# Attention scores in three units a batch instead of four, q in two transfers instead of four, and a new order of the work

## The chip, the cores and the metric

The kernel runs on one core of a Trainium2 chip. The core has a matrix engine (TensorE, PE in the profile, with its weight loads as PEld), a vector engine (VectorE, DVE), a scalar engine (ScalarE, ACT) and a general engine (GpSimd, POOL); SyncE (SP) issues DMAs. Each engine works through its own list of instructions in order and waits for the others by semaphores. The results of PE land in PSUM, eight banks of 512 fp32 columns on 128 partitions. The metric is the device time of one execution in microseconds (us), as the median of several executions.

## What is computed

Two stages, for 8 batches of 576 positions. First an attention of 8 heads of 64, whose keys and values are averages over 8 neighbouring positions (so 72 of them). Then a layer of four causal attention experts of width 64 over the result, of which the best two count at each position:

```python
k_p = k.reshape(B, H, Sp, pool, D).mean(axis=3)        # pool = 8, Sp = 72
v_p = v.reshape(B, H, Sp, pool, D).mean(axis=3)
attn = softmax(scale * np.matmul(q, k_p.transpose(0, 1, 3, 2)))
x = np.matmul(attn, v_p)                               # heads side by side: (8, 576, 512)
logits = x @ w_gate                                    # top 2 of 4 experts, softmax over them
for e in range(E):
    q, k, v = x @ wq[e], x @ wk[e], x @ wv[e]
    a = softmax(np.where(causal, -1e9, scale * (q @ k.transpose(0, 2, 1))))
    out += weight_of_expert_e * (a @ v @ wo[e])
```

(Shortened; `softmax` and the last line stand for several lines of the reference.)

## The kernel before, in words

The whole program is a list of short tokens, `SEQ` (from line 550), written out by a planner and replayed at the end of the kernel. A token is a name, its arguments, the batch, for PE work the PSUM bank (`@4`), and flags: `d` puts a read of PSUM on DVE instead of ACT, `c` cuts a PE step into four strips of 32 columns. Each engine executes its own tokens in the order of the list, so the order in `SEQ` is the order on every engine.

**Loads.** `L_q`, `L_k`, `L_v` are DMAs that POOL issues (`load`, line 114) and that convert fp32 to bf16; three raw buffers a tensor (`NRAW`). k and v come in three parts a batch, q in four: part c holds heads c and c + 4 on partitions 32c to 32c + 31. `W0` to `W4` load the weights: wq, wk, wv, the gate, wo; `c0` to `c4` copy them into order.

**First attention.** `PK` pools k on PE, `kc` copies it, `KT` transposes it, `kt` copies that into `kpT`. `U` (`turn`, line 252) transposes one head half of q on DVE into `qT`; a head half i is the four heads 4i to 4i + 3, one in each 32 partitions. `E` (`Es`, line 258) makes the scores of one head half and one half z of the positions, four heads side by side in the rows of the array and in four neighbouring banks, 288 columns each. `e` (`es`, line 268) reads the four banks and writes the exponentials into `eta` on ACT. `D` sums `eta` over the keys, `d` and `x` turn that into a reciprocal by a logarithm and an exponential on ACT. `PV`, `vc` pool v; `O` multiplies `eta` by it and `o` scales the result into `xT` on DVE. D0 and O0x take head half 0 of positions 0 to 511, D1 and O1x head half 1, D2 and O20 the last 64 positions of both.

**Experts.** `V` and `v` make the values and gate logits, `P` and `p` the queries and keys (q0, q1, k0, k1: of two experts each; t: the last 64 positions of all), `g` the gate, mostly on POOL. `S` makes expert scores, `s` their exponentials on ACT, `a` the causal mask on POOL. `B` multiplies by the values, `bz` (DVE), `bg` (POOL) and `b` (DVE) scale. `T` and `t` transpose, `Y` multiplies by wo, `y` copies into an output tile, which SP sends off (the very last tile also ACT, in two halves `ya`, `yb`).

`H` is a run of matmuls without use that keeps PE busy at the start (39 in all).

Of the kernel before, what the change touches and what calls it, by code (L numbers as in the profile page):

```python
# [20 lines left out]
def kernel(  # L21
# [12 lines left out]
    nc = tc.nc  # L34

    B, H, S, D = q.shape
# [17 lines left out]
    NRAW = 3  # L54
    KR = 96
    NRG = 4
    NTK = S // 32
    HALF = S // 2
# [12 lines left out]
    psum = psp.tile([128, 8, 512], FP32, name="psum")  # L71
# [4 lines left out]
    qraws = bufs(NRAW, [128, 2, NTK, D], BF16, "qraw")  # L76
# [3 lines left out]
    kpTs = bufs(2, [128, 2, 2, KR], BF16, "kpT")  # L80
# [33 lines left out]
    def load(b, nm, c):  # L114
        if nm == "q":
            dst = qraws[b % NRAW][32 * c : 32 * c + 32].rearrange("p e s d -> p e (s d)")
            src = q[b, c::NRG, :, :].rearrange("e (p s) d -> p e (s d)", s=NTK)
        else:
            raw, T = (kraws, k) if nm == "k" else (vraws, v)
            dst = raw[b % NRAW][:, c, :, :, :].rearrange("p h t d -> p h (t d)")  # L120
            src = T[b, :, 2 * KR * c : 2 * KR * (c + 1), :].rearrange("h (p t) d -> p h (t d)", t=2)
        nc.gpsimd.dma_start(out=dst, in_=src)  # L122
# [135 lines left out]
    def Es(b, bank, i, z):  # L258
        for u in range(2):
            for r in range(NRG):  # L260
                rows = slice(32 * r, 32 * r + 32)
                nc.tensor.matmul(  # L262
                    out=psum[0:KR, bank + r, 0 : HALF].rearrange("j (s x) -> j s x", s=NTK),
                    lhsT=kpTs[b % 2][rows, u, i, :], rhs=qTs[b % 2][rows, i, :, 16 * z : 16 * z + 16, u],
                    start=(u == 0), stop=(u == 1), tile_position=(32 * r, 0),
                )

    def es(b, bank, dve, i, z):
        nc.scalar.activation(  # L269
            out=etas[b % 2][:, NRG * i : NRG * i + NRG, HALF * z : HALF * z + HALF].rearrange(  # L270
                "j r (x s) -> j r x s", s=NTK),
            in_=psum[0:KR, bank : bank + NRG, 0 : HALF].rearrange("j r (s x) -> j r x s", s=NTK),
            func=EXP, scale=ATT_EXP_SCALE,
        )
# [260 lines left out]
    def z(b, c, queue):  # L535
# [15 lines left out]
        I:0 L_k1:0 L_k2:0 L_k0:0 J:0 K:0 H16:0@7 PK:0@2 kc:0 H4:0@7 KT:0@7 kt:0 L_q2:0 L_q3:0 L_q0:0  # L551
        L_q1:0 U0:0 H7:0@6 E00:0@4 L_q1:1 L_k2:1 L_k0:1 L_k1:1 L_q3:1 L_q0:1 e00:0 E01:0@0 U1:0
        E11:0@4 e01:0 D0:0@0 e11:0 d0:0 x0:0 PK:1@1 kc:1d L_q2:1 E10:0@4 H2:0@3 KT:1@2 e10:0 H4:0@3
        D1:0@4 kt:1 U1:1 E10:1@0 L_v2:0 d1:0 L_v1:0 H2:0@7 E11:1@4 e10:1 U0:1 E01:1@0 e11:1 e01:1
        D2:0@4 d2:0 L_v0:0 PV:0@5 W3:0 vc:0 D1:1@6 E00:1@0 x1:0 M:0 H1:0@7 O11:0@5 O01:0@4 o11:0
        d1:1 L_v0:1 e00:1 L_v1:1 O10:0@7 o10:0 O00:0@6 o00:0 L_v2:1 PV:1@5 vc:1 W0:0 D0:1@2 c0:0d
        H3:0@7 O20:1@5 W1:0 L_k1:2 W2:0 o01:0 x2:0 O11:1@6 d0:1 c1:0 c2:0d O00:1@3 O01:1@0 x0:1
        o00:1 D2:1@2 d2:1 O10:1@1 o01:1 x1:1 x2:1 L_k2:2 c3:0 P_q0:0@4c o20:1 p_q0:0 P_k0:0@2c
        O20:0@3 o20:0 p_k0:0 o10:1 P_q1:0@7c o11:1 L_k0:2 c4:0 L_q1:2 S00:0@2 P_t0:0@5c L_q0:2
        P_k1:0@4c L_q3:2 L_q2:2 p_t0:0d L_q1:3 V1:0@5c p_q1:0d PK:2@7 s00:0 p_k1:0 S12:0@3 S10:0@1  # L560
        kc:2d L_k1:3 V0:0@6 L_k0:3 v1:0d s12:0 v0:0d L_k2:3 KT:2@7 V2:0@0 kt:2d U0:2 L_q3:3 L_v1:2
        s10:0 L_q2:3 L_q0:3 S03:0@3 s03:0 L_k1:4 V3:0@5 v3:0 L_v0:2 S02:0@6 v2:0d L_v2:2 g0:0 g1:0
        E01:2@1 V0:1@5 P_k0:1@0 e01:2 E00:2@1 s02:0 v0:1d L_v1:3 p_k0:1d P_k1:1@5 U1:2 p_k1:1d e00:2
        S11:0@6 PK:3@0 L_v0:3 E10:2@1 s11:0 a00:0 kc:3d P_q1:1@5c L_v2:3 e10:2 D0:2@0 p_q1:1d KT:3@6
        E11:2@1 L_q1:4 a11:0 L_k2:4 P_t0:1@7 d0:2 L_k0:4 V4:1@0 V1:1@5 kt:3d L_q2:4 U0:3 p_t0:1d
        v1:1d e11:2 E00:3@1 x0:2 L_q3:4 v4:1 S01:0@6 V2:1@0 V3:1@5 U1:3 g2:0 v2:1d e00:3 E10:3@1
        s01:0 v3:1d L_q0:4 e10:3 L_q1:5 PV:2@0 D2:2@5 D1:2@6 d1:2 g1:1 d2:2 L_v0:4 P_q0:1@7c x1:2
        E01:3@1 e01:3 L_v1:4 vc:2d L_q0:5 O11:2@0 p_q0:1d o11:2 S12:1@5 L_k2:5 O00:2@7 O10:2@0
        L_k0:6 o00:2 D0:3@1 s12:1 o10:2 g3:0 O01:2@2 o01:2 g4:0 g5:0 g6:0 L_v2:4 d0:3 PV:3@3 E11:3@4
        x2:2 vc:3d L_v2:6 g7:0 S10:1@0 P_q1:2@2c p_q1:2d e11:3 L_k2:6 a01:0 a03:0 g8:0 s10:1 a10:0  # L570
        O20:2@3 S03:1@4 s03:1 D1:3@6 x0:3 o20:2 PK:4@7 kc:4d S01:1@0 s01:1 g2:1 g3:1 g4:1 a12:1
        S00:1@4 V2:2@3 v2:2d P_t0:2@2 V3:2@7 KT:4@3 s00:1 S11:1@0 p_t0:2d d1:3 L_q3:5 P_k0:2@2 s11:1
        U0:4 g0:1 kt:4d E00:4@3 a01:1 v3:2d e00:4 g5:1 g6:1 O01:3@7 D2:3@0 d2:3 P_k1:2@1c L_k0:5
        p_k0:2d x1:3 O00:3@2 g9:0 o01:3 O10:3@7 p_k1:2 g7:1 L_q1:6 E01:4@3 L_q0:6 U1:4 a12:0
        P_q0:2@0c g8:1 O11:3@1 a02:0 o10:3 e01:4 V1:2@7c o00:3 E11:4@3 V0:2@2c o11:3 V1:3@1c p_q0:2d
        L_q2:5 x2:3 L_k1:5 L_q3:7 e11:4 L_q3:6 a11:1 v0:2d v1:3d v1:2d V2:3@0c O20:3@2 g9:1 E10:4@3
        v2:3d e10:4 o20:3 B11:0@1 bz11:0 B01:0@7 bz01:0 bg01:0 B10:0@2 bg11:0 S02:1@3 S03:2@5 s03:2
        P_k0:3@0c s02:1 bz10:0 bg10:0 b10:0 D1:4@5 L_q2:7 V0:3@6c a00:1 L_k1:6 L_v2:5 PV:4@2 PK:5@3
        d1:4 L_v0:5 p_k0:3 v0:3 b11:0 U1:5 S12:2@4 s12:2 x1:4 b01:0 L_v1:5 vc:4d kc:5d S02:2@0
        S10:2@6 s10:2 a02:1 V3:3@2 V4:3@3 v4:3d B00:0@4 s02:2 bz00:0 bg00:0 v3:3d P_k1:3@5 T1:0@3  # L580
        D0:4@6 d0:4 a10:1 g0:3 PK:6@2 D2:4@7 L_v1:7 d2:4 b00:0 S01:2@0 s01:2 t1:0d S11:2@3 T0:0@6
        t0:0 a03:1 B11:1@7 kc:6d s11:2 p_k1:3d B01:1@2 x0:4 a02:2 x2:4 KT:5@5 g1:2 g2:2 P_q0:3@0
        bz11:1 bz01:1 P_t0:3@1 kt:5d E11:5@3 bg11:1 b11:1 p_t0:3 bg01:1 L_q2:6 B00:1@7 p_q0:3d b01:1
        L_v2:7 e11:5 S02:3@0 s02:3 g3:2 g1:3 g2:3 P_q1:3@2 bz00:1 bg00:1 U0:5 b00:1 a10:2 p_q1:3d
        g0:2 a01:2 E01:5@3 g4:2 L_q1:7 KT:6@7 kt:6d O00:4@0 o00:4 g3:3 g4:3 S01:3@1 O01:4@7 e01:5
        o01:4 L_k2:7 L_v0:6 L_k1:7 s01:3 E00:5@3 e00:5 O10:4@0 o10:4 S00:2@1 s00:2 O20:4@7 o20:4
# [110 lines left out]
```

## Time and profile before

| | us |
|---|---|
| median of 8 executions | 171.14 (170.43 to 172.31) |
| the profiled execution | 172.1 |
| its span on the core | 170.4 |
| first use of k on PE | 8.36 |
| first score on PE | 12.60 |
| first projection (`P_q0:0`) on PE | 29.57 |
| last matmul ends | 165.29 |
| ACT reads of scores (line 269) | 32, busy 35.8, mean 1132 ns |
| score matmuls (line 262) | 256, busy 15.4 |
| q issues on POOL | 32, busy 17.5, mean 550 ns |

The profile is of one execution. Its page gives busy times of each engine, a row of digits for each engine over 40 slices of the span (9 is 90% or more), the chain of work that ended last, and groups of instructions: line, engine, operation, tiles, count, then busy time and mean, then idle time before them and what ended it. The timeline lists instructions in order of time: start, duration, engine, line, and in square brackets the idle time before it and its cause. The table by stages gives the busy time of PE, PEld, DVE, ACT and POOL in a stretch (number of instructions in brackets), then the granted clock of PE, and DMA's share and rate.

The DMA queue of the loads moved 15.21 MB (counted as written). PE's idle time by stages: 6.7 us in the first 30 us, 5.0 between 30 and 100 us, none from 100 to 165 us.

### The profile page before, as it was taken

To read this page: it belongs to the slowest core of one execution; us is meant where nothing else is said; L and a number is where in the kernel's file an instruction comes from. 1 tells how busy PE (TensorE), PEld (TensorE's weight loads), DVE (VectorE), ACT (ScalarE), POOL (GpSimd) and SP (SyncE) were. 2 spreads that over 40 slices of the span, in tenths; PEclk is the share of its full clock that TensorE was granted. 3 is DMA by queue.
4 is the path that set the end of the run, shared out by engine and by line. 5 is a ranking of instruction groups with operands and counts; after the bars stand their busy time and mean duration, and the time that the engine had idled before them with its cause. 6 is when DMAs were issued, how large, how long until landed. Compare 5 with 4: busy or idle time off the path is not lost.

```text
span 170.4 us, 6329 instructions
## 1 busy us (share of the span) xinstructions
PE 153.6 (90%) x2625; PEld 84.0 (49%) x2625; DVE 110.7 (65%) x291; ACT 133.6 (78%) x226; POOL 108.6 (64%) x262
## 2 busy tenths in 40 slices
PE   7576979989999897979999899999999999999980
PEld 2232333444543544746546347645666675546740
DVE  1121706857778659668897587875995577868760
ACT  3029599959999994669999899889679859699880
POOL 7977873588957899988999316523405347456610
PEclk9996599999999999999999999999999999999997
DMA  2999999999999999999799901011530144377795
GB/s 23 167 177 195 177 181 180 202 185 191 182 189 195 181 128 117 148 151 149 86 100 150 162 6 67 4 62 65 206 112 0 65 123 153 105 263 290 230 339 177
DMA packets 49132, 25.05 MB, mean 147 GB/s; under 512 B 42192, under 2 KB 42448, under 8 KB 49104
## 3 DMA queue, kind: packets, MB, share of 16 engines
q0 software_dynamic: 43856, 15.21, 79.0%
q1 hardware_dynamic: 5168, 9.31, 15.4%
q8 instruction: 20, 0.33, 0.8%
q10 hardware_dynamic: 80, 0.13, 0.4%
q14 instruction: 8, 0.07, 0.1%
HBM read 30.42 MB, written 9.44 MB: 234 GB/s over the span
## 4 chain that ended last, share of the span: by engine, by line
PE 61%; POOL 12%; DMA 11%; ACT 8%; issue 3%; DVE 1%; POOLq 0%; DVEq 0%
PE psum L191 53%; DMA kraw<-in_k_dram 8%; ACT eta L269 6%; POOL kraw L122 4%; PE psum L262 4%; DMA qraw<-in_q_dram 3%; PE psum L200 3%; POOL qraw L122 2%; POOL etb L449 2%; PE psum L179 2%; ACT etb L432 2%; POOL vraw L122 1%; DVE qT L253 0%; ACT rza L295 0%; POOL Df L359 0%
## 5 line engine op out<-in xcount | busy, mean ns | idle before, releaser
L432 ACT ACTIVATE etb<-psum 128x1024 bf16<-128x1024 f32 x48 | 48.2, 1029 | 5.8 <-PE psum L191 5.0
L269 ACT ACTIVATE eta<-psum 96x1152 bf16<-96x1152 f32 x32 | 35.8, 1132 | 7.9 <-PE psum L262 7.6
L449 POOL TENSOR_SCALAR_AFFINE_SELECT etb<-etb 128x256 bf16<-128x256 bf16 x64 | 24.9, 406 | 8.0 <-ACT etb L432 7.5
L317 DVE TENSOR_TENSOR xT<-psum,rza 128x512 bf16<-128x512 f32 x32 | 20.6, 682 | 7.1 <-PE psum L191 5.2
L191 PE MATMUL psum<-wvg,xT 128*32 128x260 bf16 (+1 forms) x372 | 20.9, 275 | 1.9 <-DVE xT L317 1.2
L122 POOL DMA_DIRECT2D kraw<-in_k_dram x24 | 18.9, 792 | 4.4 <-PE psum L191 2.3
L182 DVE CAST qk<-psum 128x512 bf16<-128x512 f32 (+1 forms) x26 | 16.7, 647 | 6.8 <-PE psum L191 5.9
L191 PE MATMUL psum<-xT,wkp 128*32 128x512 bf16 (+3 forms) x308 | 20.4, 299 | 0.8 <-issue 0.8
L122 POOL DMA_DIRECT2D qraw<-in_q_dram x32 | 17.5, 550 | 5.1 <-DMA oT<-in_moe_wk_dram 1.0
L191 PE MATMUL psum<-xT,wqp 128*32 128x512 bf16 (+3 forms) x320 | 20.1, 301 | 0.6 <-issue 0.6
L122 POOL DMA_DIRECT2D vraw<-in_v_dram x24 | 18.6, 781 | 3.1 <-DMA qraw<-in_q_dram 1.3
L191 PE MATMUL psum<-wop,oT 128*128 128x512 bf16 (+2 forms) x98 | 20.1, 375 | 0.0
L191 PEld LDWEIGHTS <-etb 128*128 128x128 bf16 x480 | 17.3, 97 | 4.7 <-issue 2.0
L191 PE MATMUL psum<-vaug,etb 128*128 128x65 bf16 x480 | 19.0, 193 | 0.0
L262 PE MATMUL psum<-qT,kpT 32*96 32x288 bf16 x256 | 15.4, 317 | 2.5 <-ACT eta L269 1.4
L488 DVE TENSOR_TENSOR osc<-psum,gt 128x256 bf16<-128x256 f32 (+2 forms) x36 | 15.4, 440 | 3.1 <-POOL gt L483 3.1
L191 PE MATMUL psum<-qk 64*128 64x64 bf16 (+4 forms) x192 | 17.3, 278 | 0.1
L191 PEld LDWEIGHTS <-xT 128*32 128x32 bf16 (+1 forms) x372 | 13.9, 96 | 6.8 <-issue 4.2
L253 DVE STREAM_TRANSPOSE qT<-qraw 128x576 uint32<-128x576 uint32 x16 | 12.1, 765 | 8.0 <-DMA qraw<-in_q_dram 7.5
L483 POOL TENSOR_TENSOR gt<-rzb,G 128x4 f32<-128x4 f32 (+2 forms) x36 | 6.9, 201 | 15.1 <-DVE rzb L481 14.8
L182 DVE COPY ofin<-psum 128x512 f32<-128x512 f32 (+1 forms) x20 | 13.4, 674 | 3.4 <-PE psum L191 2.6
L191 PE MATMUL psum<-eta,vp 96*32 96x64 bf16 (+1 forms) x256 | 13.8, 288 | 0.4 <-DVE xT L317 0.3
(78 smaller groups left out, 234.4 us busy)
## 6 DMA issues: line engine op xcount, KB each, us to landing
out_dram<-ofin SPq DMA_DIRECT2D x32, 256.0 KB, 2.2
kraw<-in_k_dram POOLq DMA_DIRECT2D x24, 192.0 KB, 6.1
qraw<-in_q_dram POOLq DMA_DIRECT2D x32, 144.0 KB, 6.4
vraw<-in_v_dram POOLq DMA_DIRECT2D x24, 192.0 KB, 6.4
out_dram<-ofin SPq DMA_DIRECT2D x7, 128.0 KB, 2.3
oT<-in_moe_wq_dram POOLq DMA_DIRECT2D x1, 256.0 KB, 8.1
oT<-in_moe_wk_dram POOLq DMA_DIRECT2D x1, 256.0 KB, 8.7
oT<-in_moe_wv_dram POOLq DMA_DIRECT2D x1, 256.0 KB, 9.0
```

Of the source, the lines that this page charges most:

```text
L122: nc.gpsimd.dma_start(out=dst, in_=src)
L182: (nc.vector.tensor_copy if dve else nc.scalar.copy)(out=out, in_=in_)
L191: nc.tensor.matmul(out=out, lhsT=lhsT, rhs=rhs, start=start, stop=stop)
L200: nc.tensor.transpose(out=out[s], in_=in_[:, s], identity=ident[0:n, 0:n])
L253: nc.vector.transpose(out=qTs[b % 2][:, i].rearrange("p s x u -> p (s x u)").bitcast(U32), in_=qraws[b % NRAW][:, i].rearrange("p s d -> p ...
L262: nc.tensor.matmul(out=psum[0:KR, bank + r, 0 : HALF].rearrange("j (s x) -> j s x", s=NTK), lhsT=kpTs[b % 2][rows, u, i, :], rhs=qTs[b % 2 ...
L269: nc.scalar.activation(out=etas[b % 2][:, NRG * i : NRG * i + NRG, HALF * z : HALF * z + HALF].rearrange("j r (x s) -> j r x s", s=NTK), i ...
L317: nc.vector.tensor_tensor(out=xT[:, 2 * g + t, mcols(b)], in0=psum[:, bank, :], in1=rz[:, g, 0:MAIN], op=MULT)
L432: nc.scalar.activation(out=et[:, ep, :, eo : eo + n], in_=psum[:, bank : bank + 2, 0:n], func=EXP, scale=MOE_EXP_SCALE,)
L449: nc.gpsimd.affine_select(out=blk, in_=blk, pattern=[[0, 2], [1, 128]], compare_op=ISGE, fill=0.0, base=0, channel_multiplier=-1,)
L483: nc.gpsimd.tensor_mul(out=gt[:, :, :, 0], in0=rz[:, :, :, 0], in1=at[b // 2, "G"][:, p0:p1, 2 * ep : 2 * ep + 2].rearrange("p c e -> p e c"),
L488: nc.vector.tensor_tensor(out=oscs[ep][:, own, :].rearrange("p c (e d) -> p e c d", e=2), in0=o[:, :, :, 0:HD], in1=gt.to_broadcast([128, ...
```

## The change

Scores: the 2 x 576 columns of the two head halves are cut at columns 378 and, in the second half, 180. The first unit takes 378 columns of half 0, the second the other 198 of half 0 and 180 of half 1 side by side in the same four banks, the third the last 396 of half 1. ACT still reads four pieces a batch, of 4 x 378, 198, 180 and 396 columns; `e10` now reads what `E01` wrote. There is no `E10`.

Queries: a transfer c is head half c of all 128 partitions (288 KB as written, 144 KB before), two a batch, so that `U0` waits for one transfer and `U1` for the other.

```diff
     def load(b, nm, c):
         if nm == "q":
-            dst = qraws[b % NRAW][32 * c : 32 * c + 32].rearrange("p e s d -> p e (s d)")
-            src = q[b, c::NRG, :, :].rearrange("e (p s) d -> p e (s d)", s=NTK)
+            dst = qraws[b % NRAW][:, c].rearrange("p s d -> p (s d)")
+            src = q[b, NRG * c : NRG * c + NRG, :, :].rearrange("r (p s) d -> (r p) (s d)", s=NTK)
...
-    def Es(b, bank, i, z):
-        for u in range(2):
-            for r in range(NRG):
-                rows = slice(32 * r, 32 * r + 32)
-                nc.tensor.matmul(
-                    out=psum[0:KR, bank + r, 0 : HALF].rearrange("j (s x) -> j s x", s=NTK),
-                    lhsT=kpTs[b % 2][rows, u, i, :], rhs=qTs[b % 2][rows, i, :, 16 * z : 16 * z + 16, u],
-                    start=(u == 0), stop=(u == 1), tile_position=(32 * r, 0),
-                )
+    XCUT = {(0, 0): (0, 21), (0, 1): (21, 32), (1, 0): (0, 10), (1, 1): (10, 32)}
+    UNITS = {(0, 0): [(0, 0)], (0, 1): [(0, 1), (1, 0)], (1, 1): [(1, 1)]}
+
+    def xpart(i, z):
+        x0, x1 = XCUT[i, z]
+        off = NTK * (XCUT[0, 1][1] - XCUT[0, 1][0]) if (i, z) == (1, 0) else 0
+        return x0, x1, slice(off, off + NTK * (x1 - x0))
+
+    def Es(b, bank, *unit):
+        for i, z in UNITS[unit]:
+            x0, x1, cols = xpart(i, z)
+            for u in range(2):
+                for r in range(NRG):
+                    rows = slice(32 * r, 32 * r + 32)
+                    nc.tensor.matmul(
+                        out=psum[0:KR, bank + r, cols].rearrange("j (s x) -> j s x", s=NTK),
+                        lhsT=kpTs[b % 2][rows, u, i, :], rhs=qTs[b % 2][rows, i, :, x0:x1, u],
+                        start=(u == 0), stop=(u == 1), tile_position=(32 * r, 0),
+                    )
 
     def es(b, bank, dve, i, z):
+        x0, x1, cols = xpart(i, z)
         nc.scalar.activation(
-            out=etas[b % 2][:, NRG * i : NRG * i + NRG, HALF * z : HALF * z + HALF].rearrange(
+            out=etas[b % 2][:, NRG * i : NRG * i + NRG, NTK * x0 : NTK * x1].rearrange(
                 "j r (x s) -> j r x s", s=NTK),
-            in_=psum[0:KR, bank : bank + NRG, 0 : HALF].rearrange("j r (s x) -> j r x s", s=NTK),
+            in_=psum[0:KR, bank : bank + NRG, cols].rearrange("j r (s x) -> j r x s", s=NTK),
             func=EXP, scale=ATT_EXP_SCALE,
         )
```

The order: all of `SEQ` is planned anew. Its head and its end, old and new:

```diff
-        I:0 L_k1:0 L_k2:0 L_k0:0 J:0 K:0 H16:0@7 PK:0@2 kc:0 H4:0@7 KT:0@7 kt:0 L_q2:0 L_q3:0 L_q0:0
-        L_q1:0 U0:0 H7:0@6 E00:0@4 L_q1:1 L_k2:1 L_k0:1 L_k1:1 L_q3:1 L_q0:1 e00:0 E01:0@0 U1:0
-        E11:0@4 e01:0 D0:0@0 e11:0 d0:0 x0:0 PK:1@1 kc:1d L_q2:1 E10:0@4 H2:0@3 KT:1@2 e10:0 H4:0@3
-        D1:0@4 kt:1 U1:1 E10:1@0 L_v2:0 d1:0 L_v1:0 H2:0@7 E11:1@4 e10:1 U0:1 E01:1@0 e11:1 e01:1
-        D2:0@4 d2:0 L_v0:0 PV:0@5 W3:0 vc:0 D1:1@6 E00:1@0 x1:0 M:0 H1:0@7 O11:0@5 O01:0@4 o11:0
-        d1:1 L_v0:1 e00:1 L_v1:1 O10:0@7 o10:0 O00:0@6 o00:0 L_v2:1 PV:1@5 vc:1 W0:0 D0:1@2 c0:0d
...
-        Y3:6@6 b11:7 t02:6 bg01:7 B02:7@0 bz02:7 b01:7 Y1:7@3 y3:6 B12:7@2 t12:6 bz12:7 T11:7@1
-        bg02:7 y1:7 T01:7@4 t01:7 b02:7 Y0:7@5 y0:7 t11:7d bg12:7 b12:7 T02:7@0 t02:7d Y2:7@1 y2:7d
-        T12:7@6 t12:7 Y3:7@3 y3:7 Y4:7@4 ya4:7 yb4:7d
+        I:0 L_k1:0 L_k0:0 J:0 L_k2:0 K:0 H16:0@7 PK:0@6 kc:0 H4:0@7 KT:0@6 M:0 L_q0:0 U0:0 L_q1:0
+        kt:0d H3:0@7 E00:0@4 e00:0 U1:0 L_k1:1 L_k0:1 H1:0@3 E01:0@0 e01:0 E11:0@4 e10:0 e11:0
+        L_k2:1 PK:1@0 D0:0@3 H2:0@2 D1:0@7 kc:1d L_q1:1 d0:0 U1:1 KT:1@2 L_q0:1 L_v1:0 d1:0 kt:1d
+        D2:0@4 H2:0@6 E11:1@0 U0:1 d2:0 E00:1@4 e11:1 e00:1 L_v2:0 L_v0:0 E01:1@0 e01:1 PV:0@4 vc:0
+        H4:0@7 O11:0@7 L_k0:2 O10:0@5 O00:0@4 e10:1 D1:1@0 W3:0 x0:0 D0:1@2 o00:0 L_k1:2 L_k2:2
+        O01:0@1 o01:0 D2:1@3 W0:0 x1:0 H2:0@6 PK:2@6 o11:0 L_q1:2 kc:2 o10:0 x2:0 W2:0 c0:0 L_q0:2
+        c1:0d O20:0@4 o20:0 H4:0@1 KT:2@6 kt:2d H1:0@7 P_q1:0@7 d1:1 d2:1 W1:0 U1:2 L_v0:1 L_v2:1
+        x1:1 p_q1:0d H3:0@6 E11:2@3 d0:1 L_v1:1 e11:2 c4:0d x2:1 P_q0:0@0 p_q0:0 U0:2 V2:0@2 V0:0@7
+        v2:0 L_k2:3 V3:0@1 L_k1:3 E01:2@3 v0:0d c3:0d L_k0:3 V1:0@7 x0:1 e10:2 L_q1:3 v3:0d e01:2
+        P_k1:0@2 c2:0d L_v2:2 P_t0:0@1 L_q0:3 v1:0 p_t0:0 E00:2@3 P_k0:0@7c D1:2@1 p_k1:0d p_k0:0d
+        e00:2 d1:2 PV:1@2 D0:2@3 d0:2 L_v1:2 S01:0@6 vc:1d S11:0@0 L_v0:2 O00:1@4 o00:1 L_k2:4 s01:0
...
+        bg12:7 b12:7 a12:7 bg02:7 b02:7 bz01:7 B11:7@2 bg01:7 Y0:7@0 t02:6d bz11:7 bg11:7 b01:7
+        T12:7@3 T02:7@1 t02:7d y3:6 Y1:7@4 t12:7d y0:7 Y4:7@5 b11:7 T11:7@3 t11:7 y1:7d ya4:7 yb4:7d
+        T01:7@2 t01:7d Y3:7@2 y3:7 Y2:7@7 y2:7
```

In the new list, PE has the same steps but for the scores (24 instead of 32) and `H` (42 matmuls instead of 39). Between ACT and DVE reads have moved: `y` on ACT 22 instead of 16, `v` 12 (10), `p` 15 (14), `kc` 2 (1), `kt` 1 (2), `t` 8 (12), weight orders `c` 1 (3); DVE has the rest. POOL issues 64 loads instead of 80.

In the replay, `e10` looks up the bank of `E01`:

```diff
-                fn(b, at[b, src, a], bool(dve), *a, **({"later": True} if later else {}))
+                fn(b, at[b, src, (0, 1) if name == "e" and a == (1, 0) else a], bool(dve), *a, **({"later": True} if later else {}))
```

## The prediction

> **What bounds the kernel now.** I read the page first: engine shares, then the slices, then the chain that ended last.
>
> ```profile
> PE 153.6 (90%) x2625; PEld 84.0 (49%) x2625; DVE 110.7 (65%) x291; ACT 133.6 (78%) x226; POOL 108.6 (64%) x262
> ...
> PE   7576979989999897979999899999999999999980
> ...
> POOL 7977873588957899988999316523405347456610
> PEclk9996599999999999999999999999999999999997
> DMA  2999999999999999999799901011530144377795
> ...
> PE 61%; POOL 12%; DMA 11%; ACT 8%; issue 3%; DVE 1%; POOLq 0%; DVEq 0%
> ```
>
> Three stages show. From slice 2 to 19 (4 to 81 us) the DMA row stands at 9: the inputs arrive as fast as the queue lets them. POOL, which issues them, is fullest from 60 to 90 us. From slice 24 on PE is full to the end; the table by stages has PE busy 10.00 of 10 us in every stretch from 100 to 160. So the time is: how late PE gets going, plus its work, plus what it loses before 100 us, plus the tail. ACT is close behind (9.81 of 10 us busy in both 40:50 and 50:60).
>
> **1. The score units on PE.** Per batch there were four units of 8 matmuls with 288 columns; there will be three, of 8 x 378, 8 x 198 + 8 x 180, and 8 x 396. Matmuls (256) and columns stay; the starts and ends of units fall from 32 to 24. A unit's price stands in the timeline of PE:
>
> ```profile
> 40.31 0.59 PE L191 MATMUL psum<-xT,wkp 128*128 128x512 bf16 x2
> 40.84 0.47 PE L262 MATMUL psum<-qT,kpT 32*96 32x288 bf16 x8
> 41.24 1.04 PE L191 MATMUL psum<-xT,wkp 128*128 128x512 bf16 x4
> ```
>
> The four of the last line run 3 steps in 1.04 - 0.38 = 0.66 us (0.38 is one's own duration), so 512 columns stream in 0.22 us and 288 in 0.12. The first line's pair has streamed by 40.31 + 0.43 = 40.74; the unit starts at 40.84 and the next work at 41.24. Two passes of 0.12 leave 0.10 us ahead of the unit and 0.16 within and behind it; its start times show 0.04 of that between the passes. A boundary thus costs 0.22 us; one goes, and one gap between passes (0.04) comes. Saved: 0.18 us a batch, 1.4 in all. Only where PE sets the pace does this count; batches 0 to 2 are scored while DMA does. I take 5.5 batches, **-1.0 us** (bounds 0 and -1.4).
>
> On ACT the four reads a batch stay. From 128x512 in 607 ns and 96x1152 in 1132 the slope is 0.82 ns a column: 1512, 792, 720 and 1584 columns make 1.43 + 0.84 + 0.78 + 1.49 = 4.53 us, against 4 x 1.13 = 4.53. Nothing. The middle unit holds its four banks for 1.62 us instead of 1.13, but three holdings sum to the same 4.5: nothing, in the sum. The unit E01 now needs both halves of qT, a new wait; in batch 0, E11, PK:1 and D0 queue behind it on PE.
>
> **2. The start.** Now the first turn waits for all four q transfers:
>
> ```profile
> 11.77 1.44 DVE L253 STREAM_TRANSPOSE qT<-qraw 128x576 uint32<-128x576 uint32 x2 [6.71 <-DMA qraw<-in_q_dram]
> ...
> 12.60 0.74 PE L262 MATMUL psum<-qT,kpT 32*96 32x288 bf16 x16 [0.94 <-DVE qT L253]
> ...
> 13.12 1.13 ACT L269 ACTIVATE eta<-psum 96x1152 bf16<-96x1152 f32 x1 [2.46 <-PE psum L262]
> ```
>
> The landing marks of batch 0: third k at 8.32, the q parts at 9.24, 9.97, 10.69, 11.64, that is 0.83 us each. In the new form a transfer is one head half, twice the bytes: q0 lands at 8.32 + 1.65 = 10.0, q1 still at 11.6. Then U0 0.77, kt on DVE behind it 0.35, E00 0.5: first exponential at 11.7, 1.4 us earlier. U1 ends at 12.4, E01 at 13.0, before e00 ends at 13.2: the new wait costs nothing here, ACT covers it. M's memsets (1.3 us on DVE) now come ahead of U0, where DVE waits for q anyway. ACT then runs 4.5 us without a break, and the eta of batch 0 is whole at 16.3 against 18.6. The next gate is v of batch 0, landed at 21.1 in both orders (same bytes ahead of it); PV, vc, O and o follow at once, and the first projection starts at about 27.2 to 27.7, against 29.57.
>
> From there the bytes decide. The new order puts all of k for batch 2 and most of its q ahead of weight W1 and of v of batch 1. At the measured 0.18 MB/us W2 lands at 29.5 (30.35 before), W1 at 32.9 (27.8 before). So P_k1:0 waits until 33, and V and E01 of batch 2 fill in before it. Walking PE's order with its step times (P 0.87, V 0.45, D and O 0.22, PK 0.54), PV:1 is done at 36.5 with 15.9 us of work in old prices behind it; the old order had 14.4 at that time. Ahead by 1.5 us at most; ACT, at 9.81 of 10 from 40 us on, passes on only a part. I take **-0.8 us** (bounds 0 and -1.5).
>
> A **rule** stands against this part. The Trainium skill, "TensorE: Matmul & The Clock Gate", section on the HAM clock gate, says that the array's clock falls to half after an idle window of about 3.4 us and rises only after a busy one, the windows running freely. The trace agrees, in steps of 3.41 us:
>
> ```profile
> 7.57:10.98 3.41, 2.62 (x19) 1.18 (x19) 0.00 (x0) 1.06 (x2) 2.69 (x6) 1.00 1.09 182
> 10.98:14.39 3.41, 1.51 (x24) 0.85 (x25) 1.44 (x2) 1.27 (x2) 2.69 (x4) 1.00 1.67 175
> 14.39:17.80 3.41, 3.06 (x28) 0.93 (x28) 0.69 (x1) 3.32 (x5) 2.74 (x5) 0.50 1.38 197
> 17.80:21.22 3.42, 3.42 (x22) 1.24 (x20) 2.65 (x10) 1.48 (x3) 2.97 (x4) 0.50 1.89 177
> ```
>
> First number after the comma: PE busy; third from the end: granted clock. 1.51 us of work lost the full clock at 14.4; 3.06 did not bring it back, 3.42 did at 21.2, and the warm-up matmuls H2 and H4 were what filled that window. In the new order 17.8:21.2 holds D1, KT:1, D2, E11, E00, E01 and two warm-up matmuls, with waits for ACT between: my walk fills some 2.6 us. By the row's own clock my start stands; by the rule half clock lasts one window longer, to 24.6, and slows PV, H4 and O by some 0.5 us, which the wait for W1 then swallows. I take the walk, and keep the longer half clock as a rival.
>
> **3. Fewer transfers.** 32 q issues become 16.
>
> ```profile
> L122 POOL DMA_DIRECT2D kraw<-in_k_dram x24 | 18.9, 792 | 4.4 <-PE psum L191 2.3
> ...
> L122 POOL DMA_DIRECT2D qraw<-in_q_dram x32 | 17.5, 550 | 5.1 <-DMA oT<-in_moe_wk_dram 1.0
> ```
>
> The new transfer has 128 rows instead of 64: between 550 ns and the gate weights' 720 (256 rows); by rows, 610. 16 x 0.61 = 9.8, so POOL is relieved of 7.7 us. What does it carry to the end? Between 60 and 75 us the chain runs through POOL into a late k for batch 5:
>
> ```profile
> 73.82 0.63 PE L191 MATMUL psum<-kraw,poolk 96*32 96x512 bf16 x5 [0.97 <-DMA kraw<-in_k_dram]
> ```
>
> That 0.97 us is PE's only visible wait for a load there; q issues are 2% of the chain, 3.9 us, and 45% of that would go. So 0 to -1.8; **-0.9**, because next behind the load stand waits for xT (1.2 us) that the change does not touch. On the transfers themselves the skill ("DMA: Bandwidth & Descriptors", anatomy of one DMA on the SWDGE path) gives each about 2.0 us fixed: by it 16 fewer would free 32 us of queue. The landings say otherwise: 144 KB parts land 0.72 to 0.96 us apart, the fixed part hidden behind those in flight. I put nothing.
>
> **4. The tail.** Now the last reads are short and the PE never waits:
>
> ```profile
> 164.26 1.03 PE L191 MATMUL psum<-wop,oT 128*128 128x512 bf16 x6
> ...
> 165.38 0.42 DVE L182 COPY ofin<-psum 128x256 f32<-128x256 f32 x1 [0.29 <-PE psum L191]
> ```
>
> PE ends at 165.29, the last copy at 165.81. In the new order T01 follows Y4 and T11, and t01 stands on DVE behind y1 (0.69) and yb4 (0.42). From the start s of Y1: y1 until s+1.3, yb4 until 1.7, t01 until 2.0; PE is out of work from 1.2. Y3 runs at 2.05, Y2 at 2.5, and y3, y2 follow each other on ACT (0.59 each) until 3.8. Work ends 0.8 us later than with a full PE, and the last copy 0.3 us farther behind. **+1.1 us** (bounds 0.4 and 1.4).
>
> **5. Moves between ACT and DVE.** Six more y (0.585) go to ACT, +3.5; v +1.1, p +0.6, kc +0.6; away go t 2.4, weight orders 1.9, kt 0.5. ACT +1.0 us of 133.6, DVE -3.7 of 110.7. Priced at nothing while PE is fuller than ACT; where ACT is full it is the second rival below. Three more warm-up matmuls (42 for 39) lie in waits.
>
> **Sum.** -1.0 - 0.8 - 0.9 + 1.1 = -1.6 on a span of 170.4: 168.8. Outside the span lie 172.1 - 170.4 = 1.7, so 170.5 beside the profiled execution's 172.1; from the median of 171.14 it is **169.5**. All low bounds give -4.3, all high ones +1.4: 166.8 to 172.5.
>
> **The rivals.**
> - **Everything carries through** (0.22): start and units count in full, the POOL relief too, -1.5 - 1.4 - 1.8 + 1.1 = -3.6: 167.5. For it: PE is full from 100 us on, so what is won earlier stays. Against: ACT at 98% in the middle.
> - **ACT takes over** (0.17): between 40 and 100 us ACT runs without gaps, its list is 1.0 longer, so the -0.8 and the unit savings vanish there; -0.9 - 0.3 + 1.1, about 0: 171.0. It is also the case in which the units save nothing.
> - **Half clock lasts into the projections** (0.17), the slower case. It decides if the window 21.2:24.6 is not filled either. Then 24.6:31.4 runs at half rate; 7 us of windows do 3.5 us less, from which the -1.6 is already taken: 170.4 - 1.6 + 3.5 = 172.3 in the span, 173.0. For it: warm-ups come in pieces of 1 to 4 between waits. Against: from 21.1 v has landed and PE has O, D and PK in a row.
> - Forecast: 0.44, its own range 168.4 to 170.5.
>
> A measurement tells about 0.5% (0.86 us) from no change. Faster: the second case's 0.22 and nine tenths of the forecast, 0.62; same: the rest of the forecast and 0.13 of the ACT case, 0.17; slower 0.21. The range 166.8 to 172.0 leaves out the half-clock case and little else.
>
> **What would show it.** E units: 24, with 0.5 us from start to next. First ACT read of a score near 11.7; first projection near 27.5; P_k1:0 near 33. POOL's q row near 16 x 610. A gap of some 0.8 us on PE just before the last two Y. Wrong if the clock is half after 24.6, if PE has more idle time between 30 and 100 us than the present 5.0, or if the last Y's follow without a gap.

## The result and the profile after

The new kernel takes 169.72 us as the median of 11 executions (ten of 167.08 to 171.31 and one of 288.17, which I can't explain), the old one beside it 171.44 (169.63 to 173.69, 32 executions). The ratio is **0.9835**, 95% interval 0.9788 to 0.9882. The ratios here compare the mean of only those executions that lie within 1.5% of the quickest of their kernel (five of the new kernel's eleven), so they are not the ratios of the medians, here 0.990. A second set on another chip gave 0.9799 (0.9753 to 0.9845). The profiled execution took 166.35 us, its span 164.4, against 172.1 and 170.4 for the old kernel's. So differences between the two traces are larger than those of the medians, and I use the traces for places, the ratios for sizes.

The page of the new kernel (engine shares; slices; the chain):

```profile
PE 151.6 (92%) x2604; PEld 84.4 (51%) x2604; DVE 108.2 (66%) x287; ACT 134.1 (82%) x230; POOL 100.5 (61%) x246
...
PE   6886789999999969999999999999999999999970
...
POOL 6956667557789996759589401385940535776400
PEclk9999999999999999999999999999999999999998
DMA  2999999999999999999986910058133252587794
...
PE 70%; DMA 20%; issue 2%; ACT 2%; POOL 2%; DVE 1%; ACTq 0%; DVEq 0%; POOLq 0%
```

PE is now full from slice 15 on (62 us; slices counted from 0) instead of slice 23 (98 us), and POOL has fallen from 12% of the chain to 2%. The timeline of the new kernel has the landmarks that the prediction named:

```profile
11.43 0.56 PE L271 MATMUL psum<-qT,kpT 32*96 32x378 bf16 x8 [0.45 <-DVE kpT L181]
11.93 0.39 PE L178 MATMUL psum<-warm 128*128 128x512 bf16 x1
12.04 2.14 ACT L279 ACTIVATE eta<-psum 96x1512 bf16<-96x1512 f32 x2 [2.23 <-PE psum L271]
...
26.65 1.02 PE L190 MATMUL psum<-xT,wqp 128*128 128x512 bf16 x4
...
32.27 1.02 PE L190 MATMUL psum<-xT,wkp 128*128 128x512 bf16 x4
...
158.91 1.04 PE L190 MATMUL psum<-wop,oT 128*128 128x512 bf16 x4 [0.72 <-DVE oT L181]
```

And, from its groups, POOL's issues of q:

```profile
L121 POOL DMA_DIRECT2D qraw<-in_q_dram x16 | 9.2, 579 | 2.1 <-DMA qraw<-in_q_dram 0.9 <-DMA vraw<-in_v_dram 0.6 <-issue 0.4
```

To see where the time comes from I added up PE's steps of each trace in one set of prices (those of the old trace) and noted when a given sum was reached. Difference to the old kernel's profiled execution, in us:

| work of PE done | old at | new | two transfers alone (e2) | four by halves (e9) | loads moved (e11) | new, no later warm-up (e6) |
|---|---|---|---|---|---|---|
| 15 us | 37.3 | -2.2 | +0.2 | -0.9 | -0.2 | -0.9 |
| 30 | 54.0 | -2.8 | +0.2 | -0.6 | +0.1 | -1.7 |
| 40 | 66.6 | -3.0 | -1.8 | -0.1 | -0.8 | -3.8 |
| 50 | 77.7 | -3.7 | -3.1 | -0.4 | -1.5 | -4.5 |
| 70 | 100.8 | -6.0 | -4.0 | -0.1 | -1.1 | -5.9 |

In this execution of the new kernel 2.2 us come at the start, 3.8 between 37 and 101 us, nothing after (-6.1 at 130, -6.0 in the span). The start is not the same in every execution: e5, the same kernel once more, reaches the end of this stage 2.75 us later (see e6 and e7).

### The profile page after: what moved, and what is told of

Its sections match the earlier page's. It is cut to its first block, busy times and chain, and to the rows that moved or that the text cites. A ratio compares the mean times of both kernels' runs of the same rounds, so it can differ in the third digit from the quotient of the medians.

```text
span 164.4 us, 6279 instructions
## 1 busy us (share of the span) xinstructions
PE 151.6 (92%) x2604; PEld 84.4 (51%) x2604; DVE 108.2 (66%) x287; ACT 134.1 (82%) x230; POOL 100.5 (61%) x246
## 4 chain that ended last, share of the span: by engine, by line
PE 70%; DMA 20%; issue 2%; ACT 2%; POOL 2%; DVE 1%; ACTq 0%; DVEq 0%; POOLq 0%
PE psum L190 62%; DMA vraw<-in_v_dram 6%; DMA kraw<-in_k_dram 6%; DMA oT<-in_moe_wv_dram 5%; PE psum L271 5%; DMA qraw<-in_q_dram 4%; PE psum L199 3%; POOL kraw L121 2%; ACT etb L442 1%; ACTq L700 0%; ACT rza L309 0%; ACT rza L305 0%; ACT etb L436 0%; DVE xT L320 0%; ACT vaug L181 0%
## 5 line engine op out<-in xcount | busy, mean ns | idle before, releaser
L442 ACT ACTIVATE etb<-psum 128x1024 bf16<-128x1024 f32 x48 | 47.3, 1029 | 4.5 <-PE psum L190 3.5
L279 ACT ACTIVATE eta<-psum 96x1512 bf16<-96x1512 f32 (+3 forms) x32 | 34.9, 1126 | 6.4 <-PE psum L271 5.9
L493 POOL TENSOR_TENSOR gt<-rzb,G 128x4 f32<-128x4 f32 (+2 forms) x36 | 7.1, 202 | 24.6 <-DVE rzb L491 22.9
L190 PE MATMUL psum<-wvg,xT 128*32 128x260 bf16 (+1 forms) x360 | 22.0, 275 | 0.0
L181 DVE CAST qk<-psum 128x512 bf16<-128x512 f32 (+1 forms) x25 | 16.0, 642 | 9.0 <-PE psum L190 8.7
L190 PE MATMUL psum<-xT,wqp 128*32 128x64 bf16 (+3 forms) x296 | 19.9, 279 | 1.6 <-issue 1.6
L190 PEld LDWEIGHTS <-etb 128*128 128x128 bf16 x480 | 17.2, 97 | 4.5 <-issue 2.1
L190 PE MATMUL psum<-vaug,etb 128*128 128x65 bf16 x480 | 19.3, 193 | 0.0
L271 PE MATMUL psum<-qT,kpT 32*96 32x378 bf16 (+3 forms) x256 | 14.1, 313 | 2.1 <-ACT eta L279 1.0
L178 PE MATMUL psum<-warm 128*128 128x512 bf16 x42 | 13.5, 454 | 1.2 <-DVE onesd L149 1.2
L181 ACT COPY ofin<-psum 128x512 f32<-128x512 f32 (+1 forms) x23 | 12.8, 584 | 1.9 <-PE psum L190 1.5
L190 PEld LDWEIGHTS <-wqp 128*32 128x32 bf16 (+1 forms) x296 | 8.7, 97 | 9.8 <-issue 4.2
```

The costliest lines, as they stand in the source:

```text
L178: nc.tensor.matmul(out=psum[:, bank, :], lhsT=warm[:, 0:128], rhs=warm[:], start=True, stop=True)
L181: (nc.vector.tensor_copy if dve else nc.scalar.copy)(out=out, in_=in_)
L190: nc.tensor.matmul(out=out, lhsT=lhsT, rhs=rhs, start=start, stop=stop)
L271: nc.tensor.matmul(out=psum[0:KR, bank + r, cols].rearrange("j (s x) -> j s x", s=NTK), lhsT=kpTs[b % 2][rows, u, i, :], rhs=qTs[b % 2][ro ...
L279: nc.scalar.activation(out=etas[b % 2][:, NRG * i : NRG * i + NRG, NTK * x0 : NTK * x1].rearrange("j r (x s) -> j r x s", s=NTK), in_=psum ...
L442: nc.scalar.activation(out=et[:, ep, :, eo : eo + n], in_=psum[:, bank : bank + 2, 0:n], func=EXP, scale=MOE_EXP_SCALE,)
```

## The experiments

Each kernel was executed six times or more, beside the old one on the same chip; ratios are to that.

**e1, units alone.** The old kernel with `Es`, `es` of the new one; of the four units of a batch the second goes, the middle one stands at the third's place and the last at the fourth's. D1:6 had to move behind the new unit; all other tokens stay. One batch's tokens, shortened:

```diff
-E01:4@3 e01:4 ... E11:4@3 e11:4 ... E10:4@3 e10:4
+E01:4@3 e01:4 e10:4 ... E11:4@3 e11:4
```

> The old kernel with three score units alone: the second of the four old units goes, the middle one stands at the third's place, q still comes in four transfers, everything else keeps its old order. My theory (units, start, relief of POOL each bring a part): only the boundaries are saved, at most 1.4 us, less what D0 and the reads lose because they now wait for the middle unit: 0.990 to 1.000 of before, about 170.7 us. Rival A (the new order is the whole gain): 1.00 or a little above. In both, a unit takes about 0.5 us from start to next instead of 0.4, in 24 units.

Measured 1.0188 (1.0136 to 1.0240), slower. PE's timeline in e1:

```profile
96.88 0.61 PE L272 MATMUL psum<-qT,kpT 32*96 32x198 bf16 x16
99.08 0.40 PE L191 MATMUL psum<-eta,onesd 96*32 96x512 bf16 x4 [1.58 <-ACT eta L280]
```

After the middle unit PE has nothing ready: the sums over `eta` stand next in its list, and ACT needs two reads, not one, before they can run. That is 1.58 us at one place. In all PE idles 1.8 us more than in the old trace (1.0 of it in the first 26 us, 0.8 behind), of the 2.2 us by which the spans differ. The waits for `xT` near 57 and 65 us that the old kernel has are not there: between 60 and 80 us PE idles 0.5 us, 2.1 in the old kernel.

**e2, two transfers alone.** The old kernel with the new `load` for q, at the places of the first and third of the four. The code and the tokens of batch 0, shortened:

```diff
-            src = q[b, c::NRG, :, :]...
+            src = q[b, NRG * c : NRG * c + NRG, :, :]...
-L_q2:0 L_q3:0 L_q0:0 L_q1:0
+L_q0:0 L_q1:0
```

> The old kernel with q in two transfers a batch alone, at the places of the first and third old transfer, the half that is turned first coming first. My theory: POOL about 8 us less busy, batch 0's first exponential more than 1 us earlier, and 0.5 to 1.5 us of time: 0.991 to 0.997 of before. Rival A (order): 1.00, since the old order asks for nothing earlier.

Measured **0.9885** (0.9827 to 0.9943), faster. The gain is not at the start (table above), but between 54 and 101 us.

**e3, both, the old order.**

> Three units and two q transfers together in the old order, without the new plan. My theory: the sum of the two, 0.985 to 0.995 of before, so at least half of the gain without any new order. Rival A (order): 0.995 to 1.005, the gain is in the plan.

Measured 1.0185 (1.0103 to 1.0267): the loss of e1 stays, and its waits are the same (1.59 us for `eta` at 99.6). Two transfers give nothing on top of it, as the waits that they take away in e2 are gone in e1 already. So the new order is worth about 3.5% between e3 and the new kernel.

**e4, the new kernel with q in four.** Transfers of 64 partitions of one head half, in pairs at the places of the two; the first turn still needs half of q only.

```diff
-            dst = qraws[b % NRAW][:, c]...
+            h, w = c // 2, c % 2
+            dst = qraws[b % NRAW][64 * w : 64 * w + 64, h]...
```

> The new kernel with q in four transfers again, two of 64 partitions for each head half, at the same places, so that the first turn still waits for half of q alone: this gives POOL its 16 issues back (about 8 us busy) and changes nothing else. My theory: 0.5 to 1.8 us slower than the new kernel, 0.990 to 0.995 of before, with waits of PE for loads back between 30 and 80 us. Rival A (order): the same time as the new kernel, 0.984. Rival B (what spreads the executions is the granted clock in the first 30 us): executions of this kernel fall into the same groups by clock, some at 0.99 near 167 and some at 0.95 near 170.

Measured 0.9793 (0.9725 to 0.9861), against 0.9835 for the new kernel at first and 0.9799 for **e5**, the new kernel run once more:

> The new kernel unchanged, beside the two that follow: 0.98 to 0.99 of before by all theories. Theory C (PE's granted clock in the first 30 us spreads its executions): its time should again lie anywhere between 166 and 171 us.

So in the new order 16 more issues on POOL (17.2 us of issue instead of 9.2) cost nothing.

**e6 and e7, the clock.** e6 leaves out the 19 warm-up matmuls behind the first score unit; e7 has 8 more of them than the new kernel.

> The new kernel without the 19 warm-up matmuls that follow its first score unit (they compute nothing). Theory C (half clock lasting into the first projections costs about 3 us, as the slower rival of the prediction says): the clock row shows about half between 14 and 28 us in nearly every execution, and the time is 170 to 172 us, 1 to 3 us over the new kernel of the same call. Rival D (DMA paces PE until 33 us, so the clock there is worth nothing, and the warm-ups only stand in PE's way): the time of the new kernel, or up to 0.5 us less.

> The new kernel with 8 more warm-up matmuls before 19 us, in PE's waits between the score units (3 for 1, 4 for 2, 3 for 2, and 3 new ones). Theory C: full clock through the first 30 us in most executions, 166 to 168 us, 1 us or more under the new kernel. Rival D: no change, or up to 0.5 us more.

The table by stages of e6 (third from the end: granted clock), then of e7:

```profile
16.80:20.20 3.40, 2.72 (x28) 1.06 (x25) 1.87 (x3) 2.38 (x4) 2.21 (x3) 0.50 1.81 180
20.20:23.60 3.40, 2.00 (x26) 0.89 (x29) 0.00 (x0) 2.98 (x5) 2.10 (x4) 0.50 1.89 179
23.60:27.00 3.40, 3.40 (x37) 1.28 (x40) 1.38 (x3) 1.56 (x3) 2.52 (x4) 0.50 1.53 195
```

```profile
16.80:20.20 3.40, 3.40 (x35) 1.28 (x35) 1.73 (x3) 1.96 (x4) 2.22 (x3) 1.00 1.80 179
```

e6 runs its scores at half clock from 16.8 to 27.0 us, e7 at full clock. Measured 0.9715 (0.9661 to 0.9770) and 0.9732 (0.9689 to 0.9776): no difference between the two. The DMA columns (share, GB/s) are the same in both.

But equal end times do not price the clock here, for PE has holes that change between executions: 1.55 us at 58.4 us in the new kernel's trace, 1.57 in e7, none in e6. What prices it is one instruction followed through the traces. Here is the row of the granted clock, and DVE's copy of the pooled v of batch 1 (`vc:1`). The new kernel as first profiled, then e5:

```profile
PEclk9999999999999999999999999999999999999998
35.96 0.68 DVE L181 CAST vp<-psum 96x512 bf16<-96x512 f32 x1
```

```profile
PEclk9999678999999999999999999999999999999999
38.71 0.68 DVE L181 CAST vp<-psum 96x512 bf16<-96x512 f32 x1
```

e6, and e12 (below; up to its end the same list as e6):

```profile
PEclk9999557999999999999999999999999999999999
37.25 0.68 DVE L181 CAST vp<-psum 96x512 bf16<-96x512 f32 x1
```

```profile
PEclk9999555599999999999999999999999999999999
39.05 0.68 DVE L181 CAST vp<-psum 96x512 bf16<-96x512 f32 x1
```

e5 is the same program as the first, and differs from it by half clock at 15.9 to 19.3 and 22.8 to 26.2 us: 2.75 us at this copy, 2.0 in the span (166.4 against 164.4). In e12 half clock lasts until 33.4 us, 6.4 us longer than in e6, and costs 1.8 us. e7, at full clock and with 27 warm-up matmuls more than e6, has the copy at 36.49, 0.8 us ahead of e6. Loads do not swallow this: v of batch 1 has landed at 35.2 us in the first trace and at 35.55 in e5, 2.5 us before PE takes it up at 38.03. What remains of it at the end differs: e6's span is 163.8 us, shorter than that of either trace at full clock.

The clock changes in steps of 3.4 us (15.93, 19.34, 22.76, 26.17 in e5), as the window rule of the Trainium skill ("TensorE: Matmul & The Clock Gate", HAM clock gate) says. By the rule it falls after an idle window. The one ahead of the first fall in e5 was not empty: PE was busy for 2.11 of its 3.41 us.

**e8, two transfers, POOL filled up again.** As e2, with 16 iotas of 361 ns where the other issues stood (5.8 of the some 8 us that were taken away; POOL busy 106.1 us, 108.6 in the old kernel).

```diff
+    elif name == "F":
+        nc.gpsimd.iota(fill[:], pattern=[[-1, 256]], ...)
```

> The old kernel with q in two transfers (as in the run that measured 0.9885 of before), with an iota of 256 columns on POOL, about 0.5 us, in each of the 16 places where an issue was taken away; the iota fills a tile that nothing reads. Theory E (POOL's time in the old order makes its loads late): the gain is gone, 0.997 to 1.003 of before. Rival F (fewer, larger transfers in flight or the earlier half of q bring it): the gain stays, 0.985 to 0.992.

Measured 0.9825 (0.9791 to 0.9858): the gain stays, so it is not POOL's busy time. Two explanations were left: that the first turn needs only half of q, or that a load on POOL does more than take its 550 ns. **e9** keeps the early half and goes back to four, of 64 partitions and one head half each. They stand at the old places, the half that is turned first coming first:

```diff
-            src = q[b, c::NRG, :, :]...
+            src = q[b, NRG * h + 2 * w : NRG * h + 2 * w + 2, :, :]...
```

> The old kernel in its old order with q still in four transfers a batch, but of 64 partitions each, so that two of them make up one half of the heads and the first turn no longer waits for all four: POOL still issues 32 loads of q. Theory G: what two transfers gave the old order (0.9825 to 0.9885) is that POOL stands in front of fewer loads; a load goes out only 0.28 us after the one eight places before it has landed, and POOL's small sums stand behind it. Then this kernel gains nothing or little: 0.995 to 1.005 (170.8 to 172.5), and DVE still waits 1.5 us or more for the sums d near 56 us. Theory F: the gain is that the first turn needs half of q only. Then it gains what two transfers gave: 0.98 to 0.99, with DVE's wait for d near 56 us still there.

Measured **1.0011** (0.9986 to 1.0036): with four transfers nothing is gained. The early half is worth nothing in the old order; the number of loads is. The timeline between 50 and 58 us shows how. The old kernel:

```profile
50.52 1.57 POOL L122 DMA_DIRECT2D vraw<-in_v_dram  x2 [0.89 <-DMA qraw<-in_q_dram]
52.07 0.55 POOL L122 DMA_DIRECT2D qraw<-in_q_dram  x1
53.48 1.55 POOL L122 DMA_DIRECT2D kraw<-in_k_dram  x2 [0.85 <-DMA qraw<-in_q_dram]
56.33 0.20 POOL L372 TENSOR_TENSOR d<-W 128x8 f32<-128x8 f32 x1
56.56 0.16 DVE L376 SCALAR_TENSOR_TENSOR den<-d 128x4 f32<-128x4 f32 x1 [1.90 <-POOL d L372]
57.78 0.38 PE L191 MATMUL psum<-wvg,xT 128*128 128x260 bf16 x2 [0.74 <-DVE xT L310]
```

Two transfers (e2):

```profile
50.40 1.59 POOL L122 DMA_DIRECT2D vraw<-in_v_dram  x2 [0.23 <-issue]
51.97 1.54 POOL L122 DMA_DIRECT2D kraw<-in_k_dram  x2
54.81 0.20 POOL L372 TENSOR_TENSOR d<-W 128x8 f32<-128x8 f32 x1
55.05 0.16 DVE L376 SCALAR_TENSOR_TENSOR den<-d 128x4 f32<-128x4 f32 x1 [0.18 <-POOL d L372]
```

Four by halves (e9):

```profile
52.38 0.55 POOL L123 DMA_DIRECT2D qraw<-in_q_dram  x1
53.24 1.57 POOL L123 DMA_DIRECT2D kraw<-in_k_dram  x2 [0.32 <-DMA qraw<-in_q_dram]
56.11 0.20 POOL L373 TENSOR_TENSOR d<-W 128x8 f32<-128x8 f32 x1
56.35 0.16 DVE L377 SCALAR_TENSOR_TENSOR den<-d 128x4 f32<-128x4 f32 x1 [2.65 <-POOL d L373]
57.57 0.61 PE L192 MATMUL psum<-wvg,xT 128*128 128x260 bf16 x4 [1.49 <-DVE xT L311]
```

Read each from its last line back. PE waits for `xT`; DVE, which scales into `xT`, stands before that at the gate's sum `d`; POOL computes `d` late because the loads ahead of it in its list wait. Which landing? The rows name q, but a part of q lands just then by chance. In all fourteen traces a load goes out no earlier than 0.28 us after the landing of the load eight places before it, and where a load has waited it is 0.28 us after it or, with a second semaphore wait in front, 0.56. The load at 50.52 follows a part of v by 0.57 us (landed 49.94), the one at 53.48 a part of k by 0.56 (52.91), eight places before each. So POOL stands still for 0.89 and 0.85 us and issues a part of q (0.55) in between, all ahead of `d`, and DVE and PE wait in line behind it. With two transfers a batch (e2) there is one load fewer ahead, the eighth load back is an older one that has landed, and the same `d` comes 1.5 us earlier.

**e11, the three loads moved.** The old kernel, nothing changed but:

```diff
-L_v1:4 vc:2d L_q0:5 ... L_k2:5 ... L_k0:6 ... g6:0 L_v2:4
+L_v1:4 vc:2d ... g6:0 L_q0:5 L_k2:5 L_k0:6 L_v2:4
```

> The old kernel with nothing changed but the places of three loads on POOL: the part of q and two parts of k that stand ahead of the sums d of batch 0 (at 52.07, 53.48 and 54.25 us) are issued right behind them. Theory G (POOL's small sums stand behind loads that wait for a landing): DVE's wait of 1.90 us for d at 56.56 falls to under 0.5, TensorE's waits for xT at 57.78 (0.74) and 65.61 (1.16) go or fall below 0.4 each, and the whole is 0.988 to 0.995 (0.9 to 2.0 us less). Theory F (the size or earlier half of the transfers): same within 0.3%, 0.997 to 1.003, TensorE then waits elsewhere for q or k.

Measured 0.9973 (0.9940 to 1.0006): theory G expected 0.9 to 2.0 us less, and some 0.5 came, at most 1.0. The number is theory F's, but F has fallen with e9, and the trace shows half of what G said. In e11:

```profile
53.76 0.20 POOL L372 TENSOR_TENSOR d<-W 128x8 f32<-128x8 f32 x1
...
56.71 0.62 PE L191 MATMUL psum<-wvg,xT 128*128 128x260 bf16 x4
...
63.16 0.17 DVE L376 SCALAR_TENSOR_TENSOR den<-d 128x5 f32<-128x5 f32 x1 [1.90 <-POOL d L372]
64.70 0.63 PE L191 MATMUL psum<-wvg,xT 128*32 128x260 bf16 x16 [1.14 <-DVE xT L317]
```

The first `d` is 2.6 us earlier, and the waits at 57.78 and for k at 73.82 are gone. But the moved loads now stand ahead of the next batch's `d`, and the second wait (1.16 us at 65.61) stays. PE is 1.1 to 1.5 us ahead at work 50 to 70; of the whole, the interval reaches from 1.0 us less to nothing, so how much of that lasts stays open. So loads ahead of `d` make these waits; that the waits are the whole gain of e2 is not shown.

**e10, the new kernel with the old division of q**: four transfers that each carry a part of both halves, in pairs at the places of the two. In batches 0, 1, 5, 6 and 7, where a turn stands between these places, the second pair goes ahead of that turn.

```diff
-            dst = qraws[b % NRAW][:, c]...
+            dst = qraws[b % NRAW][32 * c : 32 * c + 32]...
```

> The new kernel in its new order, but with the old division of q: four transfers a batch that each carry a quarter of both halves, issued in pairs at the places of the two, so each turn needs all that has been asked for of both halves before the first turn. This takes the early half away and doubles the loads. If the early half was worth what the prediction put at the start (0.8 us), the first exponential moves from about 12.0 to 14 or later and the whole is 0.985 to 0.99 (0.5 to 1.0% above the new kernel). If the start isn't what the new kernel gains by, the first exponential moves but the whole stays within 0.978 to 0.984.

Measured 1.0588 (1.0514 to 1.0663), far beyond what was expected, and not at the start alone: at work 8 it is 5.1 us behind the old kernel, at work 60 9.5 us. DVE stands 12.5 us in all in front of turns for q; at 82 us alone 5.4, since the new order issues the second half late and now the first turn needs it too. The clock also fell once more behind that wait, to half from 87.6 to 94.5 us. It shows that the new order depends on the early half; it does not measure what the start was worth.

**e12, the end reordered**, on top of e6:

```diff
-Y4:7@5 b11:7 T11:7@3 t11:7 y1:7d ya4:7 yb4:7d T01:7@2 t01:7d Y3:7@2
+b11:7 T11:7@3 t11:7 y1:7d T01:7@2 Y4:7@5 t01:7d ya4:7 yb4:7d Y3:7@2
```

> The new kernel without the 19 warm-up matmuls behind the first score unit, and with the end reordered: the last two transposes go ahead of the fifth output block of batch 7, and the copy of the last transpose ahead of the two half copies of that block, so that the block fills the hole of 0.72 us ahead of the last two output blocks. Theory of the end (the hole is on the path): 0.4 to 0.6 us less than without the reordering (0.9715 there): 0.967 to 0.970, and no gap over 0.3 us on TensorE in the last 8 us. Rival: the two half copies, now late, end last, and the time is the same, 0.970 to 0.974.

Measured 0.9806 (0.9756 to 0.9855), so no gain over e6 (on another chip) is to be seen. The hole of 0.72 us gave way to one of 0.28 ahead of the transposes, but from the end of the last scaling to that of the last copy it takes 3.2 us instead of 2.9: the time is as the rival said, though not for its reason, for the half copies do not end last. The end is a chain of reads.

## Why the prediction was right, and where it was wrong

169.5 was forecast and 169.72 measured, 1.6 us less and 1.7 by the medians. That this fits so closely is luck: the terms were off, and the median lies among executions of very different clock. The direction and the places of the gain were right, the sizes were not.

**Score units.** The trace gives 0.50, 0.53 and 0.50 us from the start of a unit to the next work, 1.53 together against 4 x 0.40 before; with one leading gap of 0.10 less, 0.17 us a batch, 0.18 forecast. That middle units cost nothing ("three holdings sum to the same 4.5") was wrong for the old order: there the units lose 1.9% (e1). What bites, in the largest of the new waits, is not the sum of the holdings but that one consumer has to wait for two reads in a row. The new order puts other work there, and its trace has no such wait. What the units are worth in it was not measured: no run has the new order with four units.

**The start.** In the profiled execution: first exponential at 12.04 (11.7 forecast), first projection 26.65 (27.2 to 27.7), P_k1:0 at 32.27 (33), PV:1 done at 35.9 (36.5). So the step was right there, and better than forecast (-2.2 at work 15, up to -1.5 forecast). In e5 the first exponential is as early (12.05), but the first projection starts at 29.60, where the old kernel has 29.57, and P_k1:0 at 35.02. So the start's gain comes only where the clock stays full.

**The clock rival** was not wrong in its mechanism. "Wrong if the clock is half after 24.6" was a sign named beforehand, and in e5 it is half until 26.2. The forecast had put the price at 0.5 us "which the wait for W1 then swallows"; W1 landed at 32.30 in e5, and PE, busy all the while, came to P_k1:0 2.7 us later. The rival's own price was too high: it has 3.5 us for some 7 us of half clock, and 6.4 us cost 1.8 (e12 against e6). Its 173.0 lies above every execution but the one of 288.17. The granted clock of each execution points the same way: of the new kernel's, those with a mean of 0.989 to 0.997 took 166.4 to 168.2 us, those with 0.950 to 0.978 169.1 to 171.3; a mean of 0.950 makes, as an estimate, 2 x 0.050 x 168 = 17 us of half clock. It is not the only thing that spreads them, since e7 has one of 170.2 us at 0.988.

**ACT takes over** falls: between 70 and 110 us PE is busy 10.00 of 10 with ACT at 9.1 to 9.95.

**Fewer transfers** is the term with the wrong mechanism. 579 ns an issue was near (610), and the place was right: 60 to 75 us. But I charged POOL's busy time and one wait for k (0.97), and set the waits for `xT` aside as something "that the change does not touch". They are most of what changed in e2's trace: 0.74 + 1.16 + 0.97 us, all three gone. That they carry to the end in full is not shown, as e11 took two of them away for 1.0 us at most. Two transfers alone are worth 1.2 to 1.8% (2.0 to 3.0 us) in the old order, where -0.9 was forecast and -1.8 was the bound; busy time has no part in it (e8). In the new order the term is nothing (e4): it leaves no such wait, as DVE stands 0.2 us in all for `d`, 3.7 in the old kernel. So order and transfers cure the same waits, and their gains do not add. Nor does the fixed 2.0 us of a DMA that the Trainium skill gives ("DMA: Bandwidth & Descriptors", anatomy of one DMA on the SWDGE path) appear as time of the queue: 16 fewer transfers are worth 2.0 to 3.0 us in the old order and nothing in the new one, not 32.

**The tail.** A hole of 0.72 us was there (0.8 forecast), the order of reads was as walked, and the last copy ended 0.67 us behind PE instead of 0.52. But the forecast stopped at the copy. From its end to the landing of the last output the old kernel takes 3.1 us (165.80 to 168.95) and the new one 2.4 (160.62 to 162.99): the old one sends its last tile in halves, which landed 2.7 and 2.9 us after their issue, the new one ends with a whole tile, which took 2.3. So the tail cost 0.1 us, not 1.1. That closing the hole would win it back was not claimed, and e12 shows it did not in that way.

**The sum.** In the profiled execution the start brought 2.2 us (0.8 forecast), the stretch from 37 to 101 us 3.8 (1.9, from units and POOL), and the tail cost 0.1 (1.1): all three sums were off in the same direction. In e5's trace the span is 4.0 us shorter than the old one, and all of that comes behind the start. By the ratio of the first set the whole is 2.0 to 3.6 us, against 1.6 forecast. Open is how the order's own 3.5% divide over its hundreds of moves.

## What to carry to other kernels

An engine that issues loads passes every wait of the load queue on to all small operations behind it in its list; look there when an engine waits for a tiny tile, and cut the number of loads or move them behind what others wait for, both ahead of the next sums too. A price made from busy time misses that. A clock that falls at the start is priced by following one instruction through several traces, not by the end times alone. When a unit of work gets larger to save boundaries, ask who reads its whole result next, and whether the order still has work for that time.

## What the runs showed of the hardware

POOL has at most eight loads under way in this program: eight completion semaphores go round, and no load of fourteen traces left earlier than 0.28 us after the landing of the one eight places before. In the old kernel POOL stood so 24 times, 10.5 us in all; in e2 20 times and 11.1 us. So it is not how long POOL stands, but what stands behind it in its list. And the limit is in transfers, not bytes: with q in 288 KB transfers a q load takes 8.1 us from issue to landing (median), with 144 KB 6.4, and k 7.6 instead of 6.1. The profile can name the wrong transfer for such a wait, the one that landed last.

PE shows holes without a releaser, at places that recur but with sizes that change between executions: ahead of the first projections of k at 34 to 36 us 0.82, 0.48, 0.84 and 1.62 us in four kernels (old, e2, e8, e9); in the new kernel 1.55 us at 58.4, 1.57 in e7 and none in e6. Their cause stayed open.
